# Which loads of a fused MLP are issued ahead of the opening barrier

## The chip, the cores and the metric

One core of one Trainium2 chip runs the kernel. The metric is the device time of one execution in microseconds (us); a kernel's figure is the median of several executions. The clock of the profile starts with the first recorded instruction, and its span ends with the last.

## What is computed

```
B, S, D, F = 1, 2048, 576, 4608          # bfloat16 throughout
h = jnp.einsum("bsd,df->bsf", x, w1) + b1
r = jnp.where(h > 0, h, 0)
out = jnp.einsum("bsf,fd->bsd", r * r, w2) + b2
```

It is a two-layer perceptron with a squared ReLU between the layers: 2048 rows of 576 numbers, 4608 hidden units, and 576 numbers out.

## The kernel before

The rows of x are cut into four blocks of 512 (`SB`), the hidden units into 36 tiles of 128 (`NFT`). The first layer needs x with the 576 columns on partitions. For blocks 1 to 3 the DMA transposes x while loading (`load_xT`, line 273). The four row tiles of block 0, called x0 to x3 here, are instead loaded plainly (`load_x`, line 93, 144 KB each, issued by SyncE) and TensorE transposes them by matmuls with an identity (`transpose_tile`, line 179). The first six hidden tiles of w1 are loaded in the same early stage as four chunks of 128 of the 576 rows, called k0 to k3 here (`load_quad`, line 96, 192 KB each, issued by ScalarE); the last 64 rows follow in two small loads (`load_rest`, line 105, SyncE). All later pieces of w1 (line 100), the transposing loads and w2 are issued by SyncE after these.

Three things set the order of work at the start.

First, the program opens with a barrier of all five engines. [...] A hook at the end of the build (`issue_at_barrier`, lines 123 to 137) moves the loads that open the body of SyncE and of ScalarE, and wait for nothing, up into this opening block: the first two of each engine ahead of its drain, the others between the drain and the wait for the release. On SyncE these are x0, x1 | x2, x3, on ScalarE k0, k1 | k2, k3. A second hook (lines 143 to 155) does the same with one memset of VectorE and five warming matmuls of TensorE (line 166).

Second, the body of ScalarE opens with the load of an activation table and a tiny `Relu` activation on a constant (both line 112), and then come its copies out of PSUM (`copy_psum`, line 170).

Third, the order of TensorE's early work is written out by hand (lines 220 to 261). It begins so, with `V` for VectorE and `A` for ScalarE as the engine that copies the transposed tile out of PSUM:

```
transpose_tile(0, 0, 1, V)
transpose_tile(0, 3, 1, V)
transpose_tile(0, 1, 2, A)
transpose_tile(0, NC, 1, V)
full_mm(0, 1, 0)             # x0 with k0, six matmuls (line 229)
transpose_tile(1, 0, 2, V)   # x1
transpose_tile(1, 2, 2, A)
full_mm(0, 1, 1)             # x0 with k1
full_mm(1, 1, 0)
transpose_tile(2, 0, 2, V)   # x2
```

PSUM has eight banks, handed out in turn (`bank`, and the tag "bank" in `transpose_tile`). By the order above the warming matmuls take the first, the four transpose groups of x0 the next four, and the six accumulators of `full_mm` six more; so the first transpose group of x1 gets the bank which `transpose_tile(0, 1, 2, A)` used. In the built program its first weight load waits for x1, and its first matmul waits for ScalarE's second finished instruction, which is the copy of that group (the first is the tiny activation).

After this stage TensorE runs the first layer (`a_step`, line 209) for all blocks, then the second layer (lines 322 and 336).

Of the kernel before, what the change touches and what calls it, by code (L numbers as in the profile page):

```python
# [17 lines left out]
def kernel(  # L18
# [104 lines left out]
    def issue_at_barrier(nc):  # L123
        entry, body = nc.main_func.blocks[:2]
        for engine in (mybir.EngineType.SP, mybir.EngineType.Activation):
            mine = [i for i in body.instructions if i.engine == engine and not isinstance(i, mybir.InstNoOp)]
            n = 0
            while isinstance(mine[n], mybir.InstDMACopy) and not mine[n].has_wait():
                n += 1
            assert n >= RT  # L130
            for k, i in enumerate(mine[:n]):
                wanted = mybir.InstDrain if k < 2 else mybir.InstEventSemaphore
                at = next(k for k, i in enumerate(entry.instructions) if i.engine == engine and isinstance(i, wanted))
                body.instructions.remove(i)
                entry.instructions.insert(at, i)

    nc.at_finalize(issue_at_barrier)


# [236 lines left out]
```

## Time and profile before

| | |
|---|---|
| time, median of 3 runs | 290.36 us (289.94 to 290.7) |
| profiled execution: time | 290.31 us |
| profiled execution: span of the page | 288.5 us |
| TensorE busy (matmul) | 284.5 us, 99% |
| ScalarE busy | 95.4 us, 33% |
| VectorE busy | 79.8 us, 28% |
| moved by DMA | 18.31 MB |

The 1.8 us between the profiled execution's time and its span lie around the span. In the page, PE is TensorE's matmuls, PEld its weight loads, DVE is VectorE, ACT ScalarE, POOL GpSimd and SP SyncE; SPq and ACTq are the parts of SyncE and ScalarE that issue DMAs. In a line of the timeline the first number is the start and the second the duration in us, then come engine, line of the code, operation, what is written `<-` what is read, and a count where several were merged; brackets give the idle time before and what ended it. The names of tiles are without their numbers: `w_sb` is the tensor `w2_sb`, the home of w2, whose space holds x, w1's early chunks and the transposed x until w2 comes; `ph` are the accumulators of the first layer, `tp` the transposed tiles in PSUM. A line of the issues ends with the size of one DMA and the us from issue to landing.

### The profile page before, as it was taken

What the parts mean: (1) busy time and instruction counts of PE and PEld (TensorE: products, weight loads), DVE (VectorE), ACT (ScalarE), POOL (GpSimd) and SP (SyncE); (2) the same over time, 40 slices, a digit from 0 to 9 for tenths busy, and PEclk for the clock granted to TensorE, in tenths of its full rate; (3) what the DMA queues carried; (4) which work ended last, traced back from release to release, by engine and by line L of the source; (5) the groups of instructions that cost most, each with busy time, mean ns of one, the idle gap of its engine ahead of it and who ended that gap; (6) DMA issues with size and microseconds to landing.
All of it is one profiled execution on the core that took longest, in us unless ns stands there. A gap on an engine that the chain in (4) does not pass through costs nothing.

```text
span 288.5 us, 4883 instructions
## 1 busy us (share of the span) xinstructions
PE 284.5 (99%) x2097; PEld 134.9 (47%) x2108; DVE 79.8 (28%) x200; ACT 95.4 (33%) x154; POOL 1.5 (1%) x8
## 2 busy tenths in 40 slices
PE   8999999999999999999999999999999999999996
PEld 6644444444444444444445444444444444444454
DVE  2654444544444444444420011111100111111111
ACT  3576666766666676666620000000000000000000
POOL 2000000000000000000000000000000000000000
PEclk9999999999999999999999999999999999999999
DMA  8999999920400004300000100000000000000000
GB/s 239 191 198 203 194 147 223 299 81 0 124 1 2 1 2 136 112 0 2 0 3 18 20 20 20 23 20 5 15 23 20 20 20 23 20 20 22 23 20 20
DMA packets 35381, 18.31 MB, mean 63 GB/s; under 512 B 22804, under 2 KB 35360, under 8 KB 35360
## 3 DMA queue, kind: packets, MB, share of 16 engines
q1 hardware_dynamic: 34752, 17.21, 26.7%
q10 hardware_dynamic: 576, 0.79, 0.8%
q8 instruction: 16, 0.26, 0.4%
q14 instruction: 5, 0.04, 0.1%
q0 software_dynamic: 32, 0.01, 0.0%
HBM read 12.23 MB, written 2.36 MB: 51 GB/s over the span
## 4 chain that ended last, share of the span: by engine, by line
PE 97%; DMA 1%; issue 0%; SPq 0%; DVE 0%
PE ph L209 46%; PE po L336 43%; PE pc L322 5%; PE ph L229 2%; DMA w_sb<-in_x_dram 1%; PE tp L179 0%; PE ph L260 0%; SPq L93 0%; DVE o_sb L338 0%; PE b1T_ps L255 0%
## 5 line engine op out<-in xcount | busy, mean ns | idle before, releaser
L193 ACT ACTIVATE r<-ph,b1T 128x512 bf16<-128x512 f32 x144 | 90.6, 685 | 46.0 <-PE ph L209 45.1
L209 PE MATMUL ph<-w_sb,w1h 64*128 64x512 bf16 x918 | 99.2, 376 | 0.0
L209 PEld LDWEIGHTS <-w1h 64*128 64x128 bf16 x1242 | 60.4, 94 | 73.6
L336 PE MATMUL po<-w_sb,hT 128*128 128x512 bf16 x423 | 92.9, 379 | 0.5
L336 PEld LDWEIGHTS <-hT 128*128 128x128 bf16 x432 | 42.2, 98 | 51.2 <-issue 0.4
L195 DVE TENSOR_TENSOR hT<-r 128x512 bf16<-128x512 bf16 x108 | 45.7, 425 | 52.3 <-ACT r L193 52.2
L338 DVE TENSOR_TENSOR o_sb<-po,b_bc 128x512 bf16<-128x512 f32 (+2 forms) x17 | 11.2, 660 | 116.7 <-PE po L336 109.7
L209 PE MATMUL ph<-xT,w1h 64*128 64x512 bf16 x324 | 35.1, 376 | 0.0
L336 PE MATMUL po<-w_sb,w1h 128*128 128x512 bf16 (+2 forms) x178 | 31.2, 336 | 0.1
L336 PEld LDWEIGHTS <-w1h 128*128 128x128 bf16 x180 | 16.2, 98 | 15.3
L195 DVE TENSOR_TENSOR w1h<-r 128x512 bf16<-128x512 bf16 x36 | 15.3, 425 | 19.7 <-ACT r L193 19.5
L322 PE MATMUL pc<-hT,w_sb 128*64 128x512 bf16 x108 | 15.7, 379 | 0.0
L322 PEld LDWEIGHTS <-w_sb 128*64 128x64 bf16 x144 | 8.1, 110 | 7.6 <-issue 0.4
L322 PE MATMUL pc<-w1h,w_sb 128*64 128x512 bf16 x36 | 7.9, 379 | 0.0
L229 PE MATMUL ph<-w_sb 128*128 128x128 bf16 (+1 forms) x78 | 6.9, 245 | 0.0
L229 PEld LDWEIGHTS <-w_sb 128*128 128x128 bf16 x78 | 5.8, 105 | 0.2
L324 ACT ACTIVATE oc<-pc,b2T 128x512 bf16<-128x512 f32 x2 | 1.4, 687 | 13.7 <-PE pc L322 13.7
L332 DVE COPY o_sb<-oc 128x64 bf16<-128x64 bf16 x16 | 2.8, 172 | 9.2 <-DMA oc<-oc 9.2
L172 DVE COPY w_sb<-tp 128x128 bf16<-128x128 bf16 (+2 forms) x11 | 2.6, 242 | 6.7 <-PE tp L179 6.6
L170 ACT COPY w_sb<-tp 128x256 bf16<-128x256 bf16 (+2 forms) x6 | 2.0, 333 | 4.8 <-PE tp L179 4.8
L179 PE MATMUL tp<-ident,w_sb 128*128 128x128 bf16 x20 | 3.1, 259 | 0.4 <-DMA w_sb<-in_x_dram 0.4
L166 PE MATMUL wps<-one 128*128 128x512 bf16 x5 | 2.3, 629 | 0.4 <-DVE one L141 0.4
(26 smaller groups left out, 10.4 us busy)
## 6 DMA issues: line engine op xcount, KB each, us to landing
w_sb<-in_w_dram SPq DMA_DIRECT2D x2, 1728.0 KB, 8.5
out_dram<-o_sb SPq DMA_DIRECT2D x15, 144.0 KB, 1.8
w1h<-in_w_dram SPq DMA_DIRECT2D x14, 144.0 KB, 4.4
w_sb<-in_w_dram SPq DMA_DIRECT2D x2, 864.0 KB, 7.5
w1h<-in_w_dram SPq DMA_DIRECT2D x4, 288.0 KB, 6.4
w1h<-in_w_dram SPq DMA_DIRECT2D x2, 576.0 KB, 10.5
w1h<-in_w_dram SPq DMA_DIRECT2D x2, 432.0 KB, 6.0
w_sb<-in_w_dram ACTq DMA_DIRECT2D x4, 192.0 KB, 4.2
```

The lines of the kernel that those rows point to most:

```text
L166: nc.tensor.matmul(wps[:], lhsT=ones[:, 0:P], rhs=ones[:], start=(i == 0), stop=(i == NWARM - 1))
L170: nc.scalar.copy(out=dst, in_=src)
L172: nc.vector.tensor_copy(out=dst, in_=src)
L179: nc.tensor.transpose(tp[:, k, :], xs[:, j, d0:d0 + P], ident[:])
L193: nc.scalar.activation(out=r[:], in_=bk[:], func=ACT.Relu, bias=b1T[:, ft:ft + 1], scale=1.0)
L195: nc.vector.tensor_tensor(out=hT_of(b, ft), in0=r3, in1=r3, op=ALU.mult)
L209: nc.tensor.matmul(bk[h][:], lhsT=w1h[rows, c, j * P:(j + 1) * P], rhs=xT[b][rows, place(h, c), :], start=(i == 0), stop=(i == NH - 1))
L229: nc.tensor.matmul(bk0[q][:, cols], lhsT=qn[:, c, q * P:(q + 1) * P], rhs=xT[0][:, c, cols], start=(j == 0 and c == 0), stop=False, skip_g ...
L322: nc.tensor.matmul(pc[h * H:(h + 1) * H, :], lhsT=w2(ft, DM, D), rhs=hT_of(2 * pr + h, ft), start=(ft == 0), stop=(ft == NFT - 1))
L332: nc.vector.tensor_copy(out=o_sb[:, DM:D], in_=o_tr[pr][:, jj, h * H:(h + 1) * H])
L336: nc.tensor.matmul(po[:, 0:e - a], lhsT=hT_of(b, ft)[:, jj, :], rhs=w2(ft, a, e), start=(ft == 0), stop=(ft == NFT - 1))
L338: nc.vector.tensor_tensor(out=o_sb[:, a:e], in0=po[:, 0:e - a], in1=b2_bc[:, a:e], op=ALU.add)
```

## The change

The hook `issue_at_barrier` treats the two engines differently. For SyncE all stays: x0 and x1 ahead of the drain, x2 and x3 behind it. For ScalarE only the first load, k0, is moved, ahead of the drain. The loads k1, k2 and k3 stay in the body, behind the wait for the release and the branch, and ahead of the table load.

```
             assert n >= RT
+            ahead, n = (2, n) if engine == mybir.EngineType.SP else (1, 1)
             for k, i in enumerate(mine[:n]):
-                wanted = mybir.InstDrain if k < 2 else mybir.InstEventSemaphore
+                wanted = mybir.InstDrain if k < ahead else mybir.InstEventSemaphore
```

In the built program the order on ScalarE changes from k0, k1, drain, k2, k3, wait for the release, branch, table load, activation, copies to k0, drain, wait for the release, branch, k1, k2, k3, table load, activation, copies. SyncE, TensorE, VectorE and GpSimd keep their instructions, their order and their waits.

## The prediction

> **What bounds the kernel now.** I read the busy shares first, then the chain that ended last, then the first microseconds of the timeline, then the issues there one by one.
>
> ```profile
> PE 284.5 (99%) x2097; PEld 134.9 (47%) x2108; DVE 79.8 (28%) x200; ACT 95.4 (33%) x154; POOL 1.5 (1%) x8
> ```
>
> TensorE is busy for 99% of the span, so only its few idle moments can be won or added to. The chain shows where they are:
>
> ```profile
> 0.00 0.39 SPq L93
> 0.39 0.06 issue
> 0.44 3.82 DMA w_sb<-in_x_dram
> 4.26 0.05 issue
> 4.31 0.61 PE tp L179 x4
> 4.92 0.95 PE ph L229 x12
> ```
>
> The second load of SyncE, x1, is issued at 0.44, lands at 4.26 and releases TensorE at 4.31; from there to the end the chain is TensorE with small steps. The timeline around it:
>
> ```profile
> 0.00 1.91 SPq L93 DMA_DIRECT2D w_sb<-in_x_dram  x4
> 0.12 1.94 ACTq L96 DMA_DIRECT2D w_sb<-in_w_dram  x4
> ...
> 1.41 0.20 POOL masks.py:197 MEMSET ident<- 128x128 bf16 x1 [0.96 <-POOLq L360]
> ...
> 2.16 1.28 ACT L112 ACT_TABLE_LOAD   x1 [2.16 <-ACTq L360]
> ...
> 3.16 0.80 PE L229 MATMUL ph<-w_sb 128*128 128x128 bf16 x6
> ...
> 3.46 0.20 ACT L112 ACTIVATE warm<-const-float32-1.0 128x1 f32<-128x1 f32 x1
> 3.57 0.35 ACT L170 COPY w_sb<-tp 128x256 bf16<-128x256 bf16 x1
> ...
> 4.31 0.61 PE L179 MATMUL tp<-ident,w_sb 128*128 128x128 bf16 x4 [0.35 <-DMA w_sb<-in_x_dram]
> ...
> 4.71 1.16 PE L229 MATMUL ph<-w_sb 128*128 128x128 bf16 x12
> ...
> 5.82 0.50 PE L229 MATMUL ph<-w_sb 128*128 128x128 bf16 x6
> ```
>
> Two things are to be seen. ScalarE is not free while TensorE waits: its table load starts at 2.16, as soon as its four issues are out, and its copy ends only at 3.57 + 0.35 = 3.92. That copy empties the PSUM bank which the first transposes of x1 write, so TensorE waits for x1 and for it; x1 came later by 0.34. And TensorE still runs slowly here: six matmuls take 0.80 at 3.16 and 0.50 at 5.82. Single starts are 107 ns apart until 5.39 and 56 ns after.
>
> The issues taken one by one (issued plus time to landing): x0 0.00 + 2.5 = 2.5; k0 0.12 + 2.9 = 3.0; then x1 and k1:
>
> ```profile
> w_sb<-in_x_dram SPq DMA_DIRECT2D x1, 144.0 KB, 3.8
> w_sb<-in_w_dram ACTq DMA_DIRECT2D x1, 192.0 KB, 3.9
> ```
>
> that is 0.44 + 3.8 = 4.2 and 0.54 + 3.9 = 4.4. The later ones land at 5.5 (x2), 5.7 (k2), 6.6 (x3) and 6.8 (k3).
>
> [...] each queue's loads land in order, and those of the two alternate. [...]
>
> **The change, part by part.**
>
> *The barrier.* ScalarE reports after one issue, not two. Its second issue ends at 0.54 + 0.45 = 0.99 and its third starts at 1.24, so its drain reports by 1.24. SyncE's x1 ends at 0.86 and x2 starts at 1.11, so SyncE reports by 1.11 and is now last. The release comes 0.13 earlier: GpSimd's first work after it at 1.28 instead of 1.41. The identity, ready at 1.97 while x0 lands at 2.5, gains nothing from it, nor does the small b1 load, read only at 10.6. Worth nothing.
>
> *The three issues move behind the release.* ScalarE should reach its body about when GpSimd does, 1.28 (its own wait, branch and start took 0.11 from the end of k3 at 2.05 to 2.16, so not much later). So k1 is issued at 1.28 instead of 0.54, 0.74 later. The pace of ScalarE's issues was 0.42 (k0 to k1) and 0.36 (k2 to k3); I take 0.42, since SyncE issues x2 and x3 meanwhile: k2 at 1.70, k3 at 2.12, all out at 2.54.
>
> *What is queued behind them.* The table load, the tiny activation and the copy. With about 0.05 from the last issue the table load starts at 2.59, 0.43 later than now. Its chain is fixed: from its start to the end of the copy is 3.92 - 2.16 = 1.76. The copy ends at 4.35. A matmul that waits for a copy starts 0.05 after it (VectorE's first copy ends at 3.11, the matmul it releases starts at 3.16). So the first transposes of x1 can start at 4.40, where they started at 4.31: 0.09 later, however early x1 lands. Bounds: entry to the body at 1.25 to 1.35, three issues at 0.36 to 0.45 each, 0.03 to 0.11 before the table load: copy ending at 4.12 to 4.57, so x1's transposes at 4.17 to 4.62, or -0.14 to +0.31 against now.
>
> *What it takes off x1.* In its own queue k1 stands behind k0, which lands at 3.0; so it flows only after most of k0. The first bytes of x0 move 1.0 after its issue, those of k0 1.3 after its own; at this latency k1's descriptors reach the engines at 2.3 to 2.6, about when k0 runs out. So x1 loses its neighbour for perhaps 0.3 us on some engines and lands between 3.5 (two thirds of the wait gone, the lower bound) and 4.24. I take 4.0; the copy at 4.35 is later, so this gain is covered.
>
> *k1 late.* TensorE wants k1 just after the four transposes of x1, at 4.71 now and 4.80 then. It landed at 4.4. As its place in the queue is kept by k0 ahead of it, I take 4.5; if it slips by the whole 0.74, it lands at 5.2 and costs 0.5 of slow clock. k2 and k3 are issued 0.46 and 0.52 later but wait behind k1 anyway; TensorE needs them at 6.27 and 8.21, against 5.7 and 6.8: a slip of 0.5 is just covered for k2, easily for k3. Nothing.
>
> *SyncE's queue.* It waits for k0 before its fifth issue (3.07) and for the later ones in turn; k1 released the issue at 5.00, 0.6 after landing. The w1 pieces so issued land at 7.9 and later, and are first read at 11.44: 3 us of cover.
>
> *The sum.* TensorE restarts 0.09 later. Up to 5.39 it works at half clock, so the lost 0.09 is worth 0.09 x 56/107 = 0.05 at full clock; after that its starts are evenly 56 or 109 ns apart up to 10.6, with no wait that could absorb it. The profiled execution, 288.5 of span and 1.8 around it, becomes 290.31 + 0.05 = 290.36. The median of the runs stands 0.05 above that execution, so I say 290.4. Bounds of this case: 290.36 - 0.07 to 290.36 + 0.16.
>
> **The rivals.**
>
> *The load is relieved and it shows (12%).* If ScalarE enters its body early, issues fast, and x1 lands by 4.1, TensorE restarts at 4.17: 0.14 earlier, worth 0.07: 290.3. Even if the whole idle time from 3.75 to 4.31 went, it would be 0.56 x 56/107 = 0.29, so 290.1. Against it stands ScalarE's sum.
>
> *The change does nothing to x1 (15%).* k1 flows at the same time as before since k0 stands ahead of it, and the copy comes just before x1: 290.36.
>
> *k1 becomes late (8%).* [...] TensorE has its x1 and waits for k1 at up to 5.25: 0.54 of slow clock, 0.28: 290.65.
>
> *The clock steps up a window later (5%).* This is the one that ends slower. In the 3.41 us before 5.39 TensorE idled 0.07 ahead of x0 and 0.56 ahead of x1, 18%[...]. With the later restart it is 0.72, 21%. [...] the next window, 3.41 at half clock, costs 3.41/2 = 1.7: 292.0. [...]
>
> **How the numbers follow.** The forecast, 60%, gives 290.4. A difference under 0.3%, 0.87 us, is about what a measurement of this kernel can tell from no change. All cases but the last lie within it. The three runs spread over 0.76, so a median of as many is unsure by about 0.4 either way: that carries 2% under 289.49 and 1% over 291.23. With the clock's 5%: faster 0.02, same 0.92, slower 0.06. The range takes the bounds 290.1 to 290.65, widened by some 0.2 to 0.3 of that spread, and leaves the clock case out: 289.9 to 290.95.
>
> **What would show it.** Right: k1 issued near 1.3, table load near 2.6, ScalarE's first copy ending near 4.35, TensorE's four transposes of x1 released by that copy, not by the DMA, near 4.4; x1 landed before it. Wrong: the restart still released by x1; a new wait for w1 before line 229; or the step to 56 ns more than 3 us after 5.39. If the table load comes at 2.4 or earlier, the issue pace was mis-sized; if k1 starts later than 1.5, the branch was.

## The result, and the profile after

| | before | changed |
|---|---|---|
| median of 6 runs | 290.15 us (289.66 to 290.70) | 292.31 us (291.20 to 292.86) |
| profiled execution, time and span | 290.31, 288.5 us | 292.86, 291.1 us |

The ratio is 1.0067, with a 95% interval from 1.0043 to 1.0092: slower, by more than the 0.3% named above, and outside the predicted range. (The executions of the changed kernel spread over 1.7 us; why is part of the finding.)

The start of the chain that ended last, in the changed kernel (lines of the code after line 131 are one higher than before):

```profile
1.21 0.06 issue
1.27 4.21 DMA w_sb<-in_w_dram
5.48 0.05 issue
5.53 1.46 PE ph L230 x12
```

The load that holds TensorE is now one of w1, k1, issued at 1.27 and landed at 5.48. The timeline of the changed kernel around it:

```profile
0.12 2.45 ACTq L96 DMA_DIRECT2D w_sb<-in_w_dram  x4
...
1.26 0.20 POOL masks.py:197 MEMSET ident<- 128x128 bf16 x1 [0.82 <-POOLq L361]
...
2.60 1.28 ACT L112 ACT_TABLE_LOAD   x1 [2.60 <-SPq L361]
...
4.00 0.35 ACT L171 COPY w_sb<-tp 128x256 bf16<-128x256 bf16 x1
...
4.41 0.58 PE L180 MATMUL tp<-ident,w_sb 128*128 128x128 bf16 x4 [0.50 <-ACT w_sb L171]
...
5.53 1.46 PE L230 MATMUL ph<-w_sb 128*128 128x128 bf16 x12 [0.53 <-DMA w_sb<-in_w_dram]
...
10.36 0.50 PE L230 MATMUL ph<-w_sb 128*128 128x128 bf16 x6
```

Up to 4.41 all on TensorE's path is as forecast: the release 0.15 earlier (GpSimd at 1.26), the table load at 2.60, the copy ending at 4.35, the transposes of x1 released by it at 4.41. x1 had landed long before, at 0.44 + 2.9 = 3.3 (the forecast had 4.0). Then comes a second wait, for k1. And TensorE stays at half clock for much longer: twelve matmuls take 1.46 at 5.53, and the starts of single ones go from 107 to 56 ns apart at 9.83, where that came at 5.39 before.

The sum closes on the two profiles. TensorE reaches line 260 (261) at 10.79 before and at 13.33 changed, 2.55 later; the two profiled executions differ by as much in time (290.31 and 292.86). Of it 0.82 is the start of `full_mm(0, 1, 1)`, 4.71 against 5.53. From there TensorE spends 0.67 us at half clock before and 4.30 changed; 3.63 us more at half clock cost 3.63 x (1 - 56/107) = 1.73. Together 2.55. One profiled execution gives this split; how it varies follows.

### The profile page after: what moved, and what is told of

Its sections match the earlier page's. It is cut to its first block, busy times and chain, and to the rows that moved or that the text cites. A ratio compares the mean times of both kernels' runs of the same rounds, so it can differ in the third digit from the quotient of the medians.

```text
span 291.1 us, 4883 instructions
## 1 busy us (share of the span) xinstructions
PE 286.4 (98%) x2097; PEld 136.4 (47%) x2108; DVE 79.8 (27%) x200; ACT 95.4 (33%) x154; POOL 1.5 (1%) x8
## 4 chain that ended last, share of the span: by engine, by line
PE 97%; DMA 1%; issue 0%; DVE 0%
PE ph L210 46%; PE po L337 43%; PE pc L323 5%; PE ph L230 2%; DMA w_sb<-in_w_dram 1%; PE tp L180 0%; PE ph L261 0%; DVE o_sb L339 0%; PE b1T_ps L256 0%
## 5 line engine op out<-in xcount | busy, mean ns | idle before, releaser
L230 PE MATMUL ph<-w_sb 128*128 128x128 bf16 (+1 forms) x78 | 8.6, 276 | 0.5 <-DMA w_sb<-in_w_dram 0.5
L230 PEld LDWEIGHTS <-w_sb 128*128 128x128 bf16 x78 | 6.9, 120 | 1.2 <-DMA w_sb<-in_w_dram 0.8
L180 PEld LDWEIGHTS <-w_sb 128*128 128x128 bf16 x20 | 2.2, 133 | 1.5 <-issue 0.7
```

The lines of the kernel that those rows point to most:

```text
L180: nc.tensor.transpose(tp[:, k, :], xs[:, j, d0:d0 + P], ident[:])
L230: nc.tensor.matmul(bk0[q][:, cols], lhsT=qn[:, c, q * P:(q + 1) * P], rhs=xT[0][:, c, cols], start=(j == 0 and c == 0), stop=False, skip_g ...
```

## The experiments

Each ratio is to executions of the kernel before on the same chip. Issue, landing and GB/s (what the DMA engines moved from 3 to 4 us) are of the one profiled execution of each run. x1's and k1's numbers in one table, for what follows:

| run | x1 landed | k1 issued | k1 landed | GB/s, 3 to 4 us | median | ratio to before (95%) |
|---|---|---|---|---|---|---|
| before | 4.26 | 0.54 | 4.46 | 353 | 290.15 | |
| changed | 3.30 | 1.27 | 5.48 | 246 | 292.31 | 1.0043 to 1.0092 |
| changed, again (e10) | 3.32 | 1.26 | 6.59 | 211 | 292.84 | (as above) |
| e1, behind the drain | 3.42 | 0.76 | 3.94 | 254 | 290.29 | 0.9994 to 1.0020 |
| e2, k2 and k3 alone moved | 3.80 | 0.54 | 4.25 | 378 | 290.15 | 0.9985 to 1.0003 |
| e3, waits filled | 3.49 | 1.26 | 5.95 | 201 | 291.28 | 1.0020 to 1.0047 |
| e4, loads as before | 3.60 | 0.54 | 4.04 | 272 | 293.82 | 1.0114 to 1.0160 |
| e5, table first | 3.55 | 1.33 | 5.73 | 227 | 292.96 | 1.0066 to 1.0105 |
| e6, loads as before | 3.52 | 0.53 | 4.01 | 286 | 290.40 | 0.9995 to 1.0015 |
| e7, loads as before | 3.55 | 0.54 | 4.06 | 322 | 291.06 | 1.0022 to 1.0057 |
| e8, x2 and x3 held | 3.44 | 1.27 | 5.34 | 68 | 294.69 | 1.0087 to 1.0164 |
| e9, k1 on SyncE | 3.33 | 1.10 | 5.74 | 195 | 292.67 | 1.0065 to 1.0101 |
| e11, three ahead | 3.56 | 0.53 | 4.10 | 335 | 290.09 | 0.9983 to 1.0001 |
| e12, k1 on SyncE, ahead of the drain | 3.42 | 0.90 | 5.55 | 216 | 291.63 | 1.0032 to 1.0061 |
| e13, drain before k0 | 3.37 | 0.61 | 4.54 | 316 | 290.57 | 1.0003 to 1.0026 |
| e14, drain before x1 | 5.21 | 0.54 | 5.46 | 279 | 290.48 | 0.9995 to 1.0019 |

In all seven profiles with k1 issued at 0.90 or later it landed at 5.34 or later. In eight of the nine with k1 issued by 0.76 it landed by 4.54; the ninth, e14, is an exception. The table also puts the profile of before in another light. Its x1 at 4.26 is a late one: in e4, e6 and e7 the loads are issued as in the kernel before, and x1 landed at 3.52 to 3.60, with k1 beside it. The line of e7 for x1, issued at 0.44:

```profile
w_sb<-in_x_dram SPq DMA_DIRECT2D x1, 144.0 KB, 3.1
```

And with these same loads the GB/s run from 272 to 353, so a difference within that range says little.

### Which of the moved loads it is (e1, e2)

e1, against the changed kernel: all four loads of ScalarE ahead of its wait again, only k0 ahead of its drain.

```
-            ahead, n = (2, n) if engine == mybir.EngineType.SP else (1, 1)
+            ahead = 2 if engine == mybir.EngineType.SP else 1
```

> Edit: ScalarE issues k0 ahead of its drain, and k1, k2 and k3 between the drain and the wait for the release. k1 is issued near 0.76 instead of 0.54 (before) or 1.27 (changed kernel); the table load stays at 2.16 and the release comes 0.13 earlier, as in the changed kernel. Theory (what costs is that k1's descriptors come after its queue has run out of k0, and the idle time so made): k1's descriptors arrive near 2.1, before k0 ends at 2.56, so k1 lands at 4.4 to 4.6, TensorE waits no longer than before, time 290.0 to 290.4. Rival (every 0.1 of later issue costs in proportion: 1.02 us of later landing for 0.73 of later issue): k1 lands near 4.75, 0.1 later than it is wanted, time 290.4 to 290.8. Rival (the earlier release or the single early issue does the harm): time near 292.3.

Measured: 290.29 against 290.33, ratio 1.0007. The release is as early as in the changed kernel, one load alone stands ahead of the drain, and no time is lost: neither the earlier release nor the single early load is what costs (one of its 14 executions took 292.26; the kernel before had none over 290.88 there). k1 was issued at 0.76 and landed at 3.94, earlier than before and than either expectation. The proportional rival falls. What was late in this profile (290.75) is x2, for which TensorE waited 0.78 us; from the chain:

```profile
1.10 4.76 DMA w_sb<-in_x_dram
5.87 0.05 issue
5.92 0.28 PE tp L180 x2
```

e2, against the changed kernel: k0 and k1 ahead of the drain, k2 and k3 in the body.

```
-            ahead, n = (2, n) if engine == mybir.EngineType.SP else (1, 1)
+            ahead, n = (2, n) if engine == mybir.EngineType.SP else (2, 2)
```

> Edit: k0 and k1 stay ahead of ScalarE's drain; only k2 and k3 are moved behind the release. k2 and k3 are issued near 1.4 and 1.8, the table load starts near 2.25. Theory (k1 alone carries the loss): k1 lands at 4.4, x1 at 4.2, time 290.0 to 290.4, as before. Rival (the later k2 and k3, or the copy behind the later table load, carry a part): copy ending at 4.0 still ahead of x1, but k2 wanted at 6.27 lands late; time 290.8 to 292.3.

Measured: 290.15 against 290.33, ratio 0.9994. Moving k2 and k3 behind the release costs nothing, as the prediction had it. The loss is k1's alone.

### Is it the copy behind the table load (e5)

Against the changed kernel: the table load and the tiny activation are put ahead of k1, k2 and k3 in the body. The core of what the hook adds:

```
+        mine = [i for i in body.instructions if i.engine == mybir.EngineType.Activation ...]
...
+        for i in mine[first:last + 1]:        # table load, tiny activation
...
+            body.instructions.remove(i)
+            body.instructions.insert(at, i)   # ahead of k1
```

> Edit: the changed kernel, with the table load and the tiny activation ahead of k1, k2 and k3 in ScalarE's body. The table load starts near 1.27 and the copy that frees the bank for x1 ends near 3.5. Theory (late k1 and the idle time): k1 is still issued near 1.3, lands near 5.5; TensorE does x1's transposes at once at 3.7 and then waits 1.4 us for k1 in one piece; time 291.8 to 292.8, as the changed kernel. Rival (the copy behind the moved issues, the step the prediction built on, carries a good part): time 290.8 to 291.6. Rival (issues queue behind the table load on ScalarE): k1 issued near 2.6, time over 293.

Two lines of the timeline of this run:

```profile
3.36 0.37 ACT L178 COPY w_sb<-tp 128x256 bf16<-128x256 bf16 x1 [0.60 <-PE tp L187]
```

```profile
3.91 0.63 PE L187 MATMUL tp<-ident,w_sb 128*128 128x128 bf16 x4
5.78 1.46 PE L237 MATMUL ph<-w_sb 128*128 128x128 bf16 x12 [1.23 <-DMA w_sb<-in_w_dram]
```

The copy ends at 3.73 and TensorE goes from x0 to x1 without a pause, and still it waits 1.23 us for k1 and the time is 292.96, just over the expected range. So the step that carried the prediction, the copy behind the moved issues, happens in the changed kernel but is not what costs: its wait is only taken over by k1's.

### Idle time and the clock (e3, e4, e6, e7, e10)

A "window" in the prediction and the expectations is a stretch of 3.41 us; steps of the clock 3.41 and 3.42 us apart are measured in e10, below. That the idle time within such a stretch decides the step at its end was the author's estimate.

e3, the changed kernel with its waits filled; e6, the same in the kernel before (five matmuls, and none at the second place):

```
+    def idle_mm(n):
+        for i in range(n):
+            nc.tensor.matmul(bk0[i % G][:, 0:P], lhsT=zero[:], rhs=ident[:], start=False, stop=False, ...)
     full_mm(0, 1, 0)
+    idle_mm(6)
     transpose_tile(1, 0, 2, V)
     transpose_tile(1, 2, 2, A)
+    idle_mm(6)
     full_mm(0, 1, 1)
```

> Edit: the changed kernel, with six matmuls with a weight tile of zeros put ahead of the transposes of x1 and six ahead of x0 with k1; they add zeros to the accumulators and keep TensorE active during its two waits (0.70 and 0.74 us). The loads stay late: k1 lands near 5.5. Theory of the clock (the idle time makes TensorE step to full clock one window later, which costs 1.7 to 2.0 of the 2.2 us): the step comes back to between 3.9 and 7.3, mostly before 6, time 290.4 to 291.0. Rival of plain delay (the lost time is the late k1 and what follows it, the clock's step only falls where it falls): no gain, 292.0 to 292.6.

The start of e3's chain:

```profile
1.26 4.68 DMA w_sb<-in_w_dram
5.95 0.05 issue
5.99 0.84 PE ph L232 x12
```

Measured: 291.28 against 290.33, 0.95 slower than before but about 1 us faster than the changed kernel, though k1 landed at 5.95, later still. In the profile the starts go to 56 ns apart at 4.36, and none of the eight times is over 291.89. So about half of the loss was the clock; the other half, near 1 us, is the wait for k1 itself (0.85 in this profile). The time missed the expected 290.4 to 291.0: the clock theory had put all but a few tenths of the loss on the clock.

> Edit: the kernel before, with five matmuls with a weight tile of zeros ahead of the transposes of x1 (they add zeros to the accumulators); they fill the 0.56 us in which TensorE waits for x1. Theory of the clock: [...] at most the odd late step goes: 289.9 to 290.4. Rival (any idle time delays the step): 289.2 to 289.8, a version faster than both.

Measured: 290.40 against 290.29, ratio 1.0005 (0.9995 to 1.0015). The profile shows that this run can't answer its question: x1 landed at 3.52 and the copy ended at 3.93, so there was hardly a wait to fill, and the five matmuls, from 3.85 to 4.39, held up transposes that e1 began at 3.98. What 0.56 us of idle time does to the clock stays open here.

e4 and e7, the kernel before with all its loads in place, but the copy for x1 held up on ScalarE:

```
+    for _ in range(12):     # e7: 6
         nc.scalar.activation(out=warm[:], in_=nc.const_aps.tensor(1.0, [P, 1], FP32), func=ACT.Relu)
```

> Edit: the kernel before, all its loads where they were, with twelve tiny activations on ScalarE instead of one, so that the copy which frees the bank for x1 ends near 5.1 and TensorE restarts near 5.2 instead of 4.3: 1.4 us idle in one piece, as much as the changed kernel has in two. Theory of the clock: the step comes about a window later, time 291.7 to 292.6. Rival of plain delay: the restart 0.86 later, of which most falls where the clock would be full anyway: 0.45 us, time 290.6.

The dose was too large: the activations wait for each other, 0.235 us each, and TensorE restarted at 6.57, not 5.2. Measured: 293.82 (1.0114 to 1.0160). It shows idle time bringing 3.5 us with all loads in place: the restart was 2.26 later than in the profile of before, and the clock was down again from 7.60 to 11.02. But it does so at more than the idle time of the changed kernel. Hence e7:

> Edit: the kernel before with six tiny activations on ScalarE instead of one; they took 0.235 us apart in the run with twelve, so the copy for x1 ends near 5.1 and TensorE restarts near 5.15, 0.84 later than before and 1.4 us idle in all, the amount of the changed kernel; no load is moved. Theory (idle time makes the clock's step late in many executions, beside the plain delay): 291.2 to 292.6. Plain delay alone (0.84 at half clock at least, at full clock at most): 290.7 to 291.15.

The timeline of e7:

```profile
5.16 0.38 PE L180 MATMUL tp<-ident,w_sb 128*128 128x128 bf16 x4 [1.03 <-ACT w_sb L171]
```

Measured: 291.06 (1.0022 to 1.0057), and the nine times stand in two groups: six at 291.03 to 291.08, three at 292.40 to 292.86. The profiled execution is of the lower group; there the clock had stepped up at 4.27, within the wait, and stayed up. That group costs the plain delay (0.75), the other 1.4 to 1.8 more. Neither expectation alone fits; both occur, one in each group.

The changed kernel a second time:

> The changed kernel once more, for a second profile and more executions. Theory (late k1 in every execution, the clock's step late in some[...]): k1 at 5.2 to 5.9 again, times in two groups, near 291.3 and at 292.2 to 292.9; a profile of the lower group has the step before 4.5, one of the upper group after 7.5. Rival (k1's lateness was one execution's chance): k1 at 4.4 to 4.8 and a time below 291.

Measured: 291.19 and 291.24, and four times from 292.81 to 293.55. With the six of the result: four of twelve executions near 291.3, eight from 292.2 to 293.6. k1 landed at 6.59 in the profiled one, later than expected, and TensorE waited 1.84 for it. That execution is of the upper group, in a way not foreseen. Its stretches (columns: stretch, its length, busy us of the five engines, granted clock of TensorE, share of DMA, GB/s):

```profile
4.30:7.60 3.30, 1.35 (x22) 1.18 (x22) 0.29 (x1) 0.43 (x2) 0.00 (x0) 1.00 0.82 247
7.70:11.00 3.30, 3.30 (x29) 2.90 (x26) 0.51 (x2) 0.37 (x1) 0.00 (x0) 0.50 0.74 167
11.20:14.00 2.80, 2.80 (x41) 2.54 (x38) 0.90 (x4) 0.90 (x3) 0.00 (x0) 1.00 1.00 196
```

The clock stepped up at 4.27, down at 7.68 and up again at 11.10: steps 3.41 and 3.42 us apart. TensorE was busy for 1.35 of the first stretch, and the whole next one ran at half clock, fully busy. e4 shows the same order, with the clock down for 3.42 us:

```profile
4.20:7.60 3.40, 1.03 (x17) 0.97 (x17) 0.29 (x1) 2.44 (x11) 0.00 (x0) 1.00 0.88 259
7.70:11.00 3.30, 3.30 (x28) 2.90 (x26) 0.58 (x2) 0.37 (x1) 0.00 (x0) 0.50 0.99 201
```

In both a stretch mostly idle came ahead of the step down and a fully busy one ahead of the step up. The first step up lies at a different time from execution to execution (9.83 and 4.27 in the two profiles of the changed kernel, 3.61 to 9.83 over the runs).

Both of these profiles are of the upper group. What a late k1 costs with the clock up early is seen in e9 (below), where the clock stepped up at 4.32 and stayed up:

```profile
5.78 0.84 PE L230 MATMUL ph<-w_sb 128*128 128x128 bf16 x12 [1.30 <-DMA w_sb<-in_w_dram]
```

That execution took 291.58, 1.3 over the median of before.

### Why k1 is so late (e8, e9, e12, e11, e13, e14)

e8, against the changed kernel: x2 and x3 held back behind k0's landing, so that nothing of x runs beside k1.

```
     for j in range(RT):
-        load_x(nc.sync, j)
+        if j < 2:
+            load_x(nc.sync, j)
         load_quad(nc.scalar, j)
...
     for h in range(2):
         load_rest(nc.sync, h)
+    for j in range(2, RT):
+        load_x(nc.sync, j)
...
-            ahead, n = (2, n) if engine == mybir.EngineType.SP else (1, 1)
+            ahead, n = (2, 2) if engine == mybir.EngineType.SP else (1, 1)
```

> Edit: the changed kernel, with SyncE's x2 and x3 held back behind the two small loads of w1's last rows and behind the landing of k0 (near 2.9), so that k1 has no x2 beside it. Theory A (k1 is late since x2 and x3, issued by then, take turns with it): k1 issued at 1.27 lands at 4.0 to 4.7; x2 lands at 5.5 or later and becomes the wait; time 290.3 to 291.5. Theory B (k1 is late by its late start alone): k1 still at 5.2 to 5.6, and x2 later still; time 292.3 to 293.3.

k1's line, of the DMAs issued near 1.27:

```profile
w_sb<-in_w_dram ACTq DMA_DIRECT2D x1, 192.0 KB, 4.1
```

k1 landed at 5.34, with hardly anything beside it but the two small loads: from 3 to 4 us the DMA engines moved 68 GB/s. So it is not bandwidth taken by x2 and x3 that makes k1 late; theory A falls. In this run 11 of k1's 128 packets took more than 0.3 us, up to 1.08; in the profile of before one did, 0.50, and the median is 65 ns in both. (x2, landing at 7.4, became a second long wait, 1.24 us; the median of 294.69 is above what either theory had.)

e9: k1 on SyncE as its third load, behind its drain. e12: the same, ahead of the drain (`ahead` 3 for SyncE).

```
-        load_quad(nc.scalar, j)
+        load_quad(nc.sync if j == 1 else nc.scalar, j)
```

> Edit: the changed kernel, with k1 issued by SyncE as its third load, behind its drain and ahead of x2 and x3 (x0, x1, k1, x2, x3), while ScalarE keeps k0 ahead and k2, k3 behind the release. k1 is issued near 1.1, only 0.16 earlier than in the changed kernel, but in a queue that still has x1 to move until about 2.9. Theory A (k1 was late since its own queue had run dry by the time it came[...]): no gap, k1 follows x1, lands at 3.9 to 4.5; x2 later than before by 0.4; time 290.2 to 291.2. Theory B (a load issued after about 1.1 lands late in any queue): k1 lands at 5.0 or later, time 292 or more.

> Edit: k1 issued by SyncE as its third load, but ahead of its drain (x0, x1, k1 | x2, x3), near 0.88 instead of 1.10 when it stood behind the drain; ScalarE as in the changed kernel with k0 ahead and k2, k3 behind the release. Theory (the moment of the issue decides, whatever the queue): k1 lands at 3.9 to 4.5, time 290.2 to 291. Rival (the queue of SyncE or the third place in it makes k1 late): k1 at 5.3 or later, time over 292.

Measured: k1 landed at 5.74 in e9 and at 5.55 in e12, 4.6 us after its issue in both; 292.67 and 291.63 (the rival of e12 had over 292). In e9 its queue had x1 to move until 3.0, so a queue run dry is not the cause: theory A of e9 falls. In e12 it was issued by 0.90 and late all the same, so a point in time between 0.90 and 1.1 is not the cause either. One between 0.76 (e1) and 0.90 would fit k1, but not x2, which was issued at 1.11 in e2 and landed at 4.64, 3.5 us later.

e11, against the kernel before: three loads of each engine ahead of its drain (`k < 3`).

> Edit: the kernel before, with three loads of each engine ahead of its drain instead of two: x2 is issued near 0.88 instead of 1.11, k2 near 1.0 instead of 1.24; the release comes near 1.55 instead of 1.3. Theory (a load issued before some point between 0.73 and 1.1 lands 3 to 4 us after its issue, a later one 4.2 us or more): x2 lands at 4.4 to 4.9 instead of 5.5, k2 below 5.3. Rival (the landing is set by the bytes ahead of it): x2 5.3 to 5.6, k2 5.5 to 5.8. Either way TensorE, which wants x2 at 5.7, gains nothing: 290.0 to 290.5; if the identity came too late through the later release, 290.6 or more.

Measured: x2, issued at 0.91, landed at 4.60, as the theory had it, and k2 at 5.4, later than it had; 335 GB/s from 3 to 4 us; 290.09 against 290.35, ratio 0.9992 (0.9983 to 1.0001), no difference. SyncE's third load can be fast, then, at the very moment at which e12's was slow. The two differ in what ScalarE had out by then, k0 and k1 against k0 alone, and in the load itself, x2's 144 KB against k1's 192; which of these counts was not tested.

e13, against the kernel before: ScalarE's drain ahead of all its loads. e14: SyncE's drain between x0 and x1.

```
-                wanted = mybir.InstDrain if k < 2 else mybir.InstEventSemaphore
+                wanted = mybir.InstDrain if k < (2 if engine == mybir.EngineType.SP else 0) else ...   # e13
+                wanted = mybir.InstDrain if k < (1 if engine == mybir.EngineType.SP else 2) else ...   # e14
```

> Edit: the kernel before, with ScalarE's drain ahead of all four of its loads (drain, k0, k1, k2, k3, wait for the release), so that no drain stands between k0 and k1. k0 near 0.3, k1 near 0.72, k2 near 1.1: k1 as late as in the run with k1 behind the drain, where DMA moved only 254 GB/s from 3 to 4 us. Theory (the drain between two loads of ScalarE opens the slow stretch): DMA over 300 GB/s from 3 to 4 us, k1 below 4.5, x2 below 5.6, time 290.0 to 290.5. Rival (the later issue alone): DMA at 200 to 270 GB/s from 3 to 4 us and one of k1, x2 later than in the kernel before by 0.4 or more.

> Edit: the kernel before, with SyncE's drain between x0 and x1 (x0, drain, x1, x2, x3), so that x1 is issued near 0.68 instead of 0.44; ScalarE as before (k0, k1, drain, k2, k3). Theory (a drain between an engine's first two loads opens the slow stretch): DMA under 270 GB/s from 3 to 4 us, x1 at 4.6 or later, time 290.7 or more. Rival (only ScalarE's second load matters, by its moment): DMA over 270 GB/s, x1 near 4.3, time 290.0 to 290.5.

Measured, e13: 316 GB/s, k1 issued at 0.61 and landed at 4.54, x2 at 5.03; 290.57, ratio 1.0015 (1.0003 to 1.0026). e14: 279 GB/s, x1 issued at 0.65, 0.2 later than before, and landed at 5.2, 1.0 later; 290.48, ratio 1.0007 (0.9995 to 1.0019), so that in most executions it cost less than in the profiled one (290.85). There k1 landed at 5.46, though it was issued at 0.54 as before.

e13 is nearer the theory of the drain than its rival, with k1 and the time just over what the theory had; in e14 x1's landing is as the theory had it, the GB/s and the time as its rival. Against the theory stand e12's k1, which had no drain of its own engine ahead of it, and e1's, which had one and was fast. And 279 and 316 GB/s both lie within the 272 to 353 of the unchanged loads. So no theory of the drain is shown, and the cause is open. What the landings show without one: x2, issued at 1.11, landed at 5.26 to 5.87 in before, both profiles of the changed kernel, e1 and e3 to e7, and at 5.03 or earlier in e2, e13 and, issued at 0.91, e11. Loads issued that late come past 5 in most profiles, and the change makes k1 one of them.

## Why the prediction was wrong, point by point

*The barrier, the three issues, the table load, the copy: right.* GpSimd goes on at 1.26 for 1.28 (1.41 before, and 1.89 in e11, with three loads of each engine ahead of its drain), issues at 1.27, 1.63 and 2.12 for 1.28, 1.70 and 2.12, table load at 2.60 for 2.59, transposes of x1 at 4.41 for 4.40, released by the copy. k2 and k3 cost nothing, as said (e2), and neither did SyncE's queue: the whole 2.55 has arisen by line 261.

*"What it takes off x1": built on a late landing.* x1 landed at 3.3, not 4.0, and below the bound of 3.5. But that k1 beside it had held x1 up was read from one execution; with the loads as before, e4, e6 and e7 have x1 at 3.5 to 3.6, so next to nothing was there to be won. And with x1 at 3.5 to 3.6 the copy, which ended at 3.92, is the later of the two, so that the 4.31 from which the prediction counts is a late restart: e1, with the copy at that place, restarted at 3.98, and against that the 4.41 of the changed kernel is 0.43 later, not 0.09. It made no difference, since e5, where the copy came early, gained nothing either, as the wait for k1 took its place.

*"k1 late": the step that failed.* "As its place in the queue is kept by k0 ahead of it, I take 4.5; if it slips by the whole 0.74, it lands at 5.2." It landed at 5.48 and 6.59, beyond the worse bound, and TensorE waited for it: the "new wait for w1 before line 229" that the prediction named as a sign of being wrong. The profile of before had a better row for it: the loads issued at the same moment, x2 at 1.11 and k2 at 1.24, took 4.4 and 4.5 to land. The prediction has k2 waiting behind k1; e8 took x2 and x3 away and k1 still needed 4.1 us. That k1 flows only once k0 has, and so keeps its place, was the author's estimate; the profile of before shows that each queue's loads landed in the order of their issue, and not what sets the time of a landing. With 1.28 + 4.5 = 5.8 the wait would have been seen. The bound was wrong in kind: it took for granted that a load can't be delayed by more than its issue is, and k1, issued 0.73 later, landed 1.02 and 2.13 later than in the profile of before.

*"The clock steps up a window later": named, but priced on the wrong idle time.* It was given 5%, on a restart 0.09 later, 0.72 us idle in 3.41. That this share decides was an estimate, and no run shows a limit for it. With the wait for k1 the 3.41 us from 3.00 to 6.41 of the profiled execution held 0.71 + 0.74 = 1.45 us idle in its two waits, 42%, and the clock was still at half up to 9.83. By their times, eight of twelve executions paid for the clock; of the two profiled, one by a late step up, one by a step back down. The rival and the late k1 were weighed as two independent cases, and came as one chain: the wait for k1 is idle time, and idle time alone, with all loads in place, was followed by the clock's step down in e4 and, by their times, by a longer stretch at half clock in three of e7's nine executions. Its price, 1.7, agrees with the 1.73 measured.

*The sum* used the step at 5.39 as a fixed point. It lies elsewhere in every other profile.

So the loss has two parts, both shown: about 1 us for the wait itself (e3; the four lower times of the changed kernel), and 1 to 2 us more in the executions in which the clock is at half speed for longer (the upper groups of e7 and e10). What is not shown is why k1 lands at 5.3 to 6.6 when it is issued at 0.90 or later, 0.9 to 2.1 us after its landing in the profile of before.

## What to carry to other kernels

For a load that is to be issued later, don't add the delay of the issue to its old landing: take the time to landing of a load that is issued at that moment now (here x2 and k2, 4.4 and 4.5 us; k1 then took 4.2 and 5.3), and test whether queueing explains it before trusting that it will shrink. Look at a landing in more than one profile before building on it: x1's 4.26 was the exception, against 3.52 to 3.60 in e4, e6 and e7. Idle time of TensorE in the first microseconds could cost twice here: in e7 the wait cost 0.75 us in six executions, and three others took 1.4 to 1.8 us more, so a rival for the wait and a rival for the clock belong in one case. And when two inputs are needed one after the other, freeing the way for the first is worth nothing if the second is then late: in e5 the copy ended at 3.73, early enough, and TensorE waited 1.23 us for k1 all the same.

## What the runs showed of the hardware

TensorE's clock stepped up, and in two profiles down again: in e10 up at 4.27, down at 7.68 and up at 11.10, steps 3.41 and 3.42 us apart; in e4 down at 7.60 and up at 11.02, 3.42 apart. Single matmuls of 128 columns started 107 ns apart below the step up and 56 ns above it (before, at 5.39; changed, at 9.83). How much of the 3.41 us ahead of a step TensorE was idle, with all gaps between the matmuls counted: 21% ahead of the step up in before (the prediction's 18% leaves out a gap of 0.10), none ahead of the one in the changed kernel, 63% (e10) and 73% (e4) ahead of the steps down. In the changed kernel the 3.41 us up to 6.41 were idle for 45%, and the clock was still at half there; in e9 the 3.41 us after the step up at 4.32 were idle for 58%, and it stayed up. These shares are of single executions.

The time to landing of one load differed by up to 2.1 us: k1 took 3.2 us from issue to landing when issued at 0.76 (e1) and 4.1 to 5.3 when issued at 1.26 or 1.27, with single packets of 0.3 to 1.1 us mostly between 3 and 5 us, on either queue and with or without x2 and x3 beside them (e9, e8). It differed unmoved as well: issued at 0.53 or 0.54, k1 took 3.5 to 3.9 in six profiles and 4.9 in e14.
